# Attention and gated MLP in fp32 halves: weight words in PSUM, weight fetches among the first pairs' loads, value pooling on GpSimd

## The chip, the cores and the metric

The kernel runs on one core of a Trainium2 chip. A core has TensorE (PE, matrix products into PSUM), VectorE (DVE), ScalarE (ACT), GpSimd (POOL) and SyncE (SP), whose queue issues all transfers here; they work side by side and wait for each other by semaphores. The metric is the device time of one execution in microseconds (us), the median of the runs.

## The reference

Two stages. The attention, for 8 batches of 8 heads, 576 tokens, 64 wide:

```python
q_d = q.reshape(B, H, Sd, 4, D).mean(axis=3)        # k_d, v_d alike, Sd = 144
out_up = np.repeat(sm_attn(q_d, k_d, v_d), 4, axis=2)
mask = np.abs(pos[:, None] - pos[None, :]) < 4
scores = np.where(mask, scale * q @ k.T, -1e9)      # softmax over these, times v
out = out_up + out_local
```

The heads side by side are the rows x (8 x 576 tokens, 512 wide) of a gated MLP:

```python
xk = mu_k * x + (1 - mu_k) * x_prev                 # xr alike with mu_r; x_prev: the token before
k = np.maximum(xk @ w_k, 0.0)                       # 512 x 1024
v = (k * k) @ w_v                                   # 1024 x 512
out = v / (1 + np.exp(-(xr @ w_r)))                 # 512 x 512
```

The weights arrive as 64-bit floats and all else is fp32.

## The kernel before

*Attention* goes by pairs of heads, 32 of them, four to a batch (n = 0 to 31). SyncE loads q and k of a pair in four pieces each (`load_raw`, tag `raw`, four buffers), four-token groups of v (`load_v4`, two buffers) and windows of v (`load_windows`, three). VectorE transposes q and k (`turn_q`, `turn_k`), GpSimd pools them over four tokens (`pool_q`, `pool_k`, tiles `qd`, `kd`), and `pool_v` adds v over four tokens into `vd`: on VectorE for pairs below `VDVE`, else on GpSimd. PE writes local and pooled scores into one PSUM tile `ps_a`, VectorE takes maxima (`score_top`, `down_top`), ACT the exponentials, GpSimd the normalizations. PE then transposes the pooled weights (`down_turn`, "transpose group") and ACT spreads the local ones into `bd` (`spread`). `av_pe` multiplies with v, into the banks `acc0`, `acc1` for pairs 0 to 3 and into `c0`, `c1` after that, and VectorE adds both parts into `xt`, the rows x of a batch. From pair 5 on one block of PE work, `run_pe` ("run n"), holds the values of pair n-1 and the scores of pair n.

*The MLP* goes by chunks of 256 tokens, 18 of them (c = 0 to 17). Chunks 0 and 1 lie in batch 0, chunk 2 needs batch 1 too. `diff` forms x minus the token before (`dx`), ACT multiplies it with `mu_k` and `mu_r` (`mix_part`, tiles `muk`, `mur`, loaded by `load_mus`), VectorE adds x (`mix_add`) and splits each into a high and a low half (`xkh`, `xkl`, `xrh`, `xrl`). PE makes `k_pe` (8 k products per chunk), `r_pe` (2) and `v_pe` (8), each as three products of halves.

*The weights* come as 20 blocks of 128 x 512 64-bit floats (`WORDER`: k0 to k7, v0 to v7, r0 to r3). Each becomes an fp32 word and then two halves: ACT scales the upper 32 bits (`weight_scale`), VectorE shifts left by 3 (`weight_shift`), puts in the upper bits of the lower word (`weight_tail`) and the sign (`weight_sign`), ACT copies the high half (`weight_high`). The low half is made by PE and ACT for the first eight (`weight_diff` in a bank `c0` or `c1`, `weight_left`), by GpSimd for the others (`weight_low`). The word lies in the SBUF tile `w32`, tag `sig`, three buffers.

*The order* of the instructions on each engine is written out beforehand: `Plan` takes tasks with a duration, a rank and dependencies, and places them one by one, the task that can start first, among equals the lower rank. Buffers are handed out in the order in which the tasks were added. Each engine works through its list in that order, so a waiting instruction holds all behind it; SyncE's list is the order of the transfers. A weight's fetch has the rank

```python
add("SP", 0.5, FETCH + i, fetch_weight, i, w=[base], dma=1.75)      # FETCH = -95.0
```

and q and k of pair n the rank `at_run[n] - 18`, which is -94, -90, -86 and -82 for pairs 0 to 3.

Of the kernel before, what the change touches and what calls it, by code (L numbers as in the profile page):

```python
# [159 lines left out]
def attention_moe(ctx: ExitStack, tc, q, k, v, mu_k, mu_r, w_k, w_v, w_r, band, ident, out):  # L162
    nc = tc.nc
    cp = ctx.enter_context(tc.tile_pool(name="const", bufs=1))
    wp = ctx.enter_context(tc.tile_pool(name="work", bufs=2))
# [57 lines left out]


    def weight_scale(i):
        w = wp.tile([P, 512], F32, tag="sig", name="w32", bufs=3)
        nc.scalar.activation(w, raws[i][:, :, 1].bitcast(F32), AF.Copy, scale=2.0 ** -112)
        part32[i] = w

    def weight_shift(i):  # L230
        wi = part32[i].bitcast(I32)
        nc.vector.tensor_scalar(out=wi, in0=wi, scalar1=3, scalar2=None, op0=ALU.logical_shift_left)  # L232

    def weight_tail(i):
        wi = part32[i].bitcast(I32)
        nc.vector.scalar_tensor_tensor(out=wi, in0=raws[i][:, :, 0], scalar=29, in1=wi,  # L236
                                       op0=ALU.logical_shift_right, op1=ALU.bitwise_or)

    def weight_sign(i):
        wi = part32[i].bitcast(I32)  # L240
        nc.vector.scalar_tensor_tensor(out=wi, in0=raws[i][:, :, 1], scalar=-2147483648, in1=wi,  # L241
                                       op0=ALU.bitwise_and, op1=ALU.bitwise_or)
# [112 lines left out]
    def pool_v(n):  # L355
        d = st[n]
        v4 = d["v4"]
        vd = wp.tile([72, 4, D], F32, tag="vd", name="vd")
# [1 line left out]
        eng.tensor_tensor(out=v4[:, :, 0:128], in0=v4[:, :, 0:128], in1=v4[:, :, 128:256], op=ALU.add)  # L360
# [566 lines left out]
```

## Time and profile before

| | |
|---|---|
| Median of three runs | 721.09 us (720.60 to 721.62) |
| The profiled execution | 722.12 us, its span 720.3 us |
| Busy in the span | PE 657.7 us (91%), VectorE 489.1 (68%), ACT 439.4 (61%), GpSimd 299.7 (42%) |
| Moved | 62.2 MB, 85 GB/s over the span |
| A weight block, `v4` of a pair | 512 KB, 288 KB |
| Mean granted clock of PE | 0.955 |

The span runs from the first to the last instruction. "Busy" is the time in which an engine executed; idle time of an engine that nothing waits for costs nothing. A row of the timeline gives start, length, engine, line, operation, result and inputs, and in brackets the idle time before it and what ended it. Lines numbered L are those of the kernel before; after the change L222 is L223, L227 is L228, the three lines of shift, tail and sign keep their numbers (L232, L236, L241), and all behind them are three higher.

### The profile page before, as it was taken

Reading aid. Unit: us, or ns where it says so; the run is one execution under the profiler, and the core shown is the slowest. Engines: PE = TensorE matmul, PEld = TensorE weight load, DVE = VectorE, ACT = ScalarE, POOL = GpSimd, SP = SyncE. Lnnn points to the kernel's source line nnn. Section 1 sums busy time; section 2 is a strip of 40 time slices with the busy share of each in tenths; the row PEclk is TensorE's granted clock in tenths of the full one; section 3 lists DMA queues with packets and bytes.
Section 4 is the critical chain, followed back from the end, with each engine's and each line's share of the span. In section 5 each row is a group of like instructions: output and inputs, shape, how many; then the busy total and the mean of one; then the engine's idle time right before and its main releaser. Section 6 shows DMA issues by size and latency. Waiting matters only on the chain.

```text
span 720.3 us, 18419 instructions
## 1 busy us (share of the span) xinstructions
PE 657.7 (91%) x7352; PEld 567.0 (79%) x7352; DVE 489.1 (68%) x863; ACT 439.4 (61%) x1095; POOL 299.7 (42%) x366
## 2 busy tenths in 40 slices
PE   3557388699999999999999999999999999999997
PEld 2334276588888888888888888888888888988986
DVE  3676799987985887588764587667866774464111
ACT  3454457577675867596665667666766675644442
POOL 4233488866435455443343274434554431000000
PEclk9786589799999999999999999999999999999999
DMA  8999883456427343433243164432451100000000
GB/s 226 203 193 221 139 131 57 85 115 126 95 57 137 64 104 76 105 65 83 59 96 69 40 102 106 101 73 78 80 119 40 52 2 31 1 30 30 0 30 30
DMA packets 221848, 62.19 MB, mean 86 GB/s; under 512 B 205122, under 2 KB 214594, under 8 KB 221762
## 3 DMA queue, kind: packets, MB, share of 16 engines
q1 hardware_dynamic: 221762, 61.01, 40.5%
q8 instruction: 58, 0.95, 0.6%
q14 instruction: 28, 0.23, 0.1%
HBM read 51.55 MB, written 9.44 MB: 85 GB/s over the span
## 4 chain that ended last, share of the span: by engine, by line
PE 77%; DVE 9%; SPq 7%; DMA 4%; POOL 2%; issue 1%; ACT 1%; DVEq 0%; POOLq 0%; ACTq 0%
PE ps_g L615 26%; PE acc L664 26%; PE ps_r L646 14%; SPq L273 6%; DMA vw<-in_v_dram 3%; PE ps_v L519 3%; PE ps_a L387 3%; PE ps_v L513 2%; DVE w L241 1%; DVE w L236 1%; DVE w L232 1%; PE ps_a L454 1%; PE ps_a L447 1%; PE ps_t L494 1%; PE ps_t L495 1%
## 5 line engine op out<-in xcount | busy, mean ns | idle before, releaser
L615 PE MATMUL ps_g<-xkh,wk 128*128 128x256 f32 x1152 | 228.8, 285 | 2.2 <-ACT xkh L602 1.5
L615 PEld LDWEIGHTS ps_g<-xkh,wk 128*128 128x128 f32 x1152 | 186.9, 191 | 8.4 <-ACT xkh L602 2.0
L664 PE MATMUL acc<-wv,kh 128*128 128x512 f32 x576 | 182.2, 398 | 0.0
L615 PE MATMUL ps_g<-xkl,wk 128*128 128x256 f32 x576 | 163.1, 283 | 2.3 <-DVE xkl L607 2.3
L634 DVE TENSOR_TENSOR kl<-kk,kh 128x256 fp32r<-128x256 f32 x119 | 65.6, 552 | 104.2 <-ACT kh L627 96.4
L620 ACT ACTIVATE kk<-ps_g 128x256 f32<-128x256 f32 x144 | 54.8, 381 | 105.1 <-PE ps_g L615 102.4
L664 PEld LDWEIGHTS acc<-wv,kh 128*128 128x128 f32 x576 | 102.5, 190 | 17.1
L615 PEld LDWEIGHTS ps_g<-xkl,wk 128*128 128x128 f32 x576 | 109.5, 190 | 6.3 <-DVE xkl L607 2.6
L664 PE MATMUL acc<-wv,kl 128*128 128x512 f32 x288 | 113.7, 395 | 0.3 <-POOL kl L634 0.3
L646 PE MATMUL ps_r<-wr,xrh 128*128 128x512 f32 x288 | 90.0, 394 | 0.3 <-DVE sig L668 0.2
L664 PEld LDWEIGHTS acc<-wv,kl 128*128 128x128 f32 x288 | 54.5, 189 | 13.2 <-POOL kl L634 0.8
L627 ACT ACTIVATE kh<-kk 128x256 fp32r<-128x256 f32 x144 | 60.2, 418 | 4.6
L626 ACT ACTIVATE kk<-kk 128x256 f32<-128x256 f32 x144 | 60.1, 418 | 4.4
L634 POOL TENSOR_TENSOR kl<-kk,kh 128x256 fp32r<-128x256 f32 x25 | 22.1, 887 | 96.3 <-PE acc L664 81.5
L461 DVE TENSOR_REDUCE mxd<-ps_a 128x3 f32<-128x432 f32 x32 | 19.4, 606 | 62.7 <-PE ps_a L387 55.4
L646 PEld LDWEIGHTS ps_r<-wr,xrh 128*128 128x128 f32 x288 | 52.5, 188 | 10.5 <-DVE sig L668 0.6
L415 POOL TENSOR_TENSOR sm<-sm,mx 128x384 f32<-128x384 f32 x28 | 26.9, 959 | 79.5 <-DVE mx L410 68.1
L646 PE MATMUL ps_r<-wr,xrl 128*128 128x512 f32 x144 | 56.2, 390 | 0.0
L471 ACT ACTIVATE ad<-ps_a,mxd 128x144 f32<-128x144 f32 x96 | 35.3, 377 | 24.0 <-DVE mxd L462 12.1
L361 POOL TENSOR_TENSOR vd<-v 72x256 f32<-72x256 f32 x28 | 23.1, 824 | 62.6 <-PE ps_v L513 61.6
L351 POOL TENSOR_TENSOR tk<-kz 64x288 f32<-64x288 f32 (+1 forms) x56 | 44.4, 792 | 9.7 <-DVE kz L324 5.7
L482 POOL TENSOR_TENSOR ad<-ad,sd 128x432 f32<-128x432 f32 x32 | 29.8, 932 | 42.5 <-DVE sd L478 32.7
(105 smaller groups left out, 1212.1 us busy)
## 6 DMA issues: line engine op xcount, KB each, us to landing
vw<-in_v_dram SPq DMA_DIRECT2D x126, 96.0 KB
qraw<-in_q_dram SPq DMA_DIRECT2D x128, 72.0 KB
kraw<-in_k_dram SPq DMA_DIRECT2D x128, 72.0 KB
v<-in_v_dram SPq DMA_DIRECT2D x32, 288.0 KB
out_dram<-sig SPq DMA_DIRECT2D x36, 256.0 KB
wk<-in_moe_w_k_dram SPq DMA_DIRECT2D x8, 512.0 KB
wv<-in_moe_w_v_dram SPq DMA_DIRECT2D x8, 512.0 KB
wr<-in_moe_w_r_dram SPq DMA_DIRECT2D x4, 512.0 KB
```

Source lines behind the costliest of these rows:

```text
L273: nc.sync.dma_start(raw[o:o + 32], src[b, 2 * p + e].rearrange("(c t) (g d) -> t c g d", t=32, g=2)[:, :, dh, :])
L351: nc.gpsimd.tensor_tensor(out=tk[h], in0=k4[:, :, 0:2], in1=k4[:, :, 2:4], op=ALU.add)
L415: nc.gpsimd.tensor_tensor(out=s3, in0=s3, in1=mx[:, :, None].broadcast_to([P, 12, 32]), op=ALU.subtract)
L471: nc.scalar.activation(ad[:, t, :], ps[:, t, :], AF.Exp, scale=1.0 / 128, bias=mx[:, t:t + 1], accum_out=sd[:, t:t + 1])
L482: nc.gpsimd.tensor_tensor(out=ad, in0=ad, in1=sd[:, :, None].broadcast_to([P, 3, 144]), op=ALU.mult)
L615: nc.tensor.matmul(ps, w_k_part(p, f, w), y[:, p, :], start=(m == 0), stop=(m == len(mm) - 1))
L620: nc.scalar.activation(kk, kq[c, f], AF.Relu)
L626: nc.scalar.activation(kk, kk, AF.Square)
L627: nc.scalar.activation(kh, kk, AF.Copy)
L634: eng.tensor_tensor(out=kl, in0=kk, in1=kh.bitcast(F32), op=ALU.subtract)
L646: nc.tensor.matmul(ps, y[:, p, P * t:P * t + P], ws[f"r{p}"][:, w, :], start=(m == 0), stop=(m == len(mm) - 1))
L664: nc.tensor.matmul(accs[c][t], x[:, P * t:P * t + P], ws[f"v{f}"][:, w, :], start=(f == 0 and m == 0), stop=(f == NF - 1 and m == 2))
```

## The change

Three things. The word is built in PSUM: `weight_scale` writes to a PSUM tile in the bank `c0` or `c1` (by the weight's number), shift and tail work there, and `weight_sign` reads it and writes the finished word to `w32` in SBUF; `weight_diff` uses the same PSUM tile again. `Plan` lets the tiles of `c0`, `c1` and `sig` be handed out in the order in which it places the tasks (`ANY`), and takes the tail and the sign out of the list of work that slows beside GpSimd's. The ranks of the fetches are a list. And `VDVE = 0` puts all of `pool_v` on GpSimd.

```diff
-VDVE = 4
+VDVE = 0
-FETCH = -95.0
+FETCH = [-93.5, -93.0, -88.6, -88.5, -81.0, -80.9, -80.8, -80.7, -60, -59, -58, -57, -36, -35, -34, -33, -12, -11, -10, -9]
-    SHARED = "weight_tail weight_sign weight_low k_low mix_add mix_low mix_part diff pool_v".split()
+    SHARED = "weight_low k_low mix_add mix_low mix_part diff pool_v".split()
+    ANY = ("c0", "c1", "sig")
-                if tile not in self.queue[tag][turn[tag]:turn[tag] + same]:
+                if tag not in self.ANY and tile not in self.queue[tag][turn[tag]:turn[tag] + same]:
     def weight_scale(i):
-        w = wp.tile([P, 512], F32, tag="sig", name="w32", bufs=3)
-        nc.scalar.activation(w, raws[i][:, :, 1].bitcast(F32), AF.Copy, scale=2.0 ** -112)
-        part32[i] = w
+        shaped[i] = pp.tile([P, 512], F32, tag=w_bank(i), name="ps_w", bufs=1)
+        nc.scalar.activation(shaped[i], raws[i][:, :, 1].bitcast(F32), AF.Copy, scale=2.0 ** -112)
...
     def weight_sign(i):
-        wi = part32[i].bitcast(I32)
-        nc.vector.scalar_tensor_tensor(out=wi, in0=raws[i][:, :, 1], scalar=-2147483648, in1=wi,
-                                       op0=ALU.bitwise_and, op1=ALU.bitwise_or)
+        part32[i] = wp.tile([P, 512], F32, tag="sig", name="w32", bufs=3)
+        nc.vector.scalar_tensor_tensor(out=part32[i].bitcast(I32), in0=raws[i][:, :, 1], scalar=-2147483648,
+                                       in1=shaped[i].bitcast(I32), op0=ALU.bitwise_and, op1=ALU.bitwise_or)
+    def w_bank(i):
+        return f"c{i % 2}"
...
-        add("SP", 0.5, FETCH + i, fetch_weight, i, w=[base], dma=1.75)
-        add("ACT", 0.67, R, weight_scale, i, r=[base], new=[(f"w{i}", "sig")])
+        add("SP", 0.5, FETCH[i], fetch_weight, i, w=[base], dma=1.75)
+        add("ACT", 0.67, R, weight_scale, i, r=[base], new=[(f"ws{i}", w_bank(i))])
```

SyncE's queue behind the constants, before (`wk0` to `wr3` are weight blocks, `qraw`, `kraw`, `v4`, `vw` loads of the pairs in turn):

```order
L222 DMA wk0_91<-in_moe_w_k_dram 128x1024
L222 DMA wk1_94<-in_moe_w_k_dram 128x1024
L273 DMA qraw_96<-in_q_dram 32x18x32 x4
L273 DMA kraw_107<-in_k_dram 32x18x32 x4
L222 DMA wk2_114<-in_moe_w_k_dram 128x1024
L222 DMA wk3_117<-in_moe_w_k_dram 128x1024
L222 DMA wv0_122<-in_moe_w_v_dram 128x1024
L222 DMA wv1_124<-in_moe_w_v_dram 128x1024
L282 DMA v4_127<-in_v_dram 72x4x256
L273 DMA qraw_130<-in_q_dram 32x18x32 x4
```

and now:

```order
L276 DMA qraw_91<-in_q_dram 32x18x32 x4
L276 DMA kraw_101<-in_k_dram 32x18x32 x4
L223 DMA wk0_108<-in_moe_w_k_dram 128x1024
L223 DMA wk1_111<-in_moe_w_k_dram 128x1024
L285 DMA v4_113<-in_v_dram 72x4x256
L276 DMA qraw_118<-in_q_dram 32x18x32 x4
L276 DMA kraw_130<-in_k_dram 32x18x32 x4
L299 DMA vw_194<-in_v_dram 32x11x64
L303 DMA vw_194<-in_v_dram 29x64
L299 DMA vw_194<-in_v_dram 32x12x64 x3
L223 DMA wk2_212<-in_moe_w_k_dram 128x1024
L223 DMA wk3_217<-in_moe_w_k_dram 128x1024
```

Two weights stood ahead of pair 0's q and six ahead of pair 1's; now none and two.

SyncE's queue around `muk` and `mur`, before:

```order
L222 DMA wr2_488<-in_moe_w_r_dram 128x1024
L296 DMA vw_495<-in_v_dram 32x12x64 x4
L222 DMA wr3_515<-in_moe_w_r_dram 128x1024
L187 DMA muk_67<-in_moe_mu_k_dram 128x4x1
L188 DMA mur_68<-in_moe_mu_r_dram 128x4x1
L273 DMA qraw_537<-in_q_dram 32x18x32 x4
L273 DMA kraw_606<-in_k_dram 32x18x32 x4
L296 DMA vw_660<-in_v_dram 32x12x64 x4
```

and now:

```order
L223 DMA wv4_577<-in_moe_w_v_dram 128x1024
L223 DMA wv5_582<-in_moe_w_v_dram 128x1024
L223 DMA wv6_590<-in_moe_w_v_dram 128x1024
L223 DMA wv7_603<-in_moe_w_v_dram 128x1024
L188 DMA muk_67<-in_moe_mu_k_dram 128x4x1
L189 DMA mur_68<-in_moe_mu_r_dram 128x4x1
L276 DMA qraw_609<-in_q_dram 32x18x32 x4
L276 DMA kraw_685<-in_k_dram 32x18x32 x4
L223 DMA wr0_713<-in_moe_w_r_dram 128x1024
L223 DMA wr1_720<-in_moe_w_r_dram 128x1024
L223 DMA wr2_724<-in_moe_w_r_dram 128x1024
L223 DMA wr3_727<-in_moe_w_r_dram 128x1024
```

The r weights stand behind q and k of pair 4 and behind `muk` and `mur`, which stand behind the sixteen k and v weights still.

VectorE at the last weight word and chunk 1's `xk` (`at`: transposed local weights; `xt` rows: the values of pair 4), before:

```order
L232 TENSOR_SCALAR w32_1456<-w32_1456 128x512
L236 SCALAR_TENSOR_TENSOR w32_1456<-wr3_515,w32_1456 128x512
L241 SCALAR_TENSOR_TENSOR w32_1456<-wr3_515,w32_1456 128x512
L552 TENSOR_TENSOR xt_105<-ps_v_1308,up_1466 128x6x48
L552 TENSOR_TENSOR xt_105<-ps_v_1309,up_1466 128x6x48
L435 STREAM_TRANSPOSE at_1523<-sm_1427 128x384
L598 TENSOR_TENSOR xk32_1167<-xk32_1167,xt_101 128x1024
L310 STREAM_TRANSPOSE qT1_77<-qraw_1201 128x576
L319 STREAM_TRANSPOSE kz1_74<-kraw_1239 128x576
L607 TENSOR_TENSOR xkl_1626<-xk32_1167,xkh_1614 128x1024
```

and now (`ps_w` are the PSUM tiles):

```order
L232 TENSOR_SCALAR ps_w_1318<-ps_w_1318 128x512
L236 SCALAR_TENSOR_TENSOR ps_w_1318<-wr2_724,ps_w_1318 128x512
L241 SCALAR_TENSOR_TENSOR w32_1346<-wr2_724,ps_w_1318 128x512
L601 TENSOR_TENSOR xk32_1089<-xk32_1089,xt_97 128x1024
L232 TENSOR_SCALAR ps_w_1344<-ps_w_1344 128x512
L236 SCALAR_TENSOR_TENSOR ps_w_1344<-wr3_727,ps_w_1344 128x512
L241 SCALAR_TENSOR_TENSOR w32_1382<-wr3_727,ps_w_1344 128x512
L610 TENSOR_TENSOR xkl_1387<-xk32_1089,xkh_1372 128x1024
L601 TENSOR_TENSOR dx_997<-dx_997,xt_97 128x1024
L464 TENSOR_REDUCE mxd_1490<-ps_a_1390 128x3
```

The values of pair 4 and pair 5's `at` came before chunk 1's `xkl`; they come later now.

PE in front of chunk 1's first k product, before (`L513`, `L519`: values of pair 5; the rows of `ps_a`: scores of pair 6; its values' banks are `c0`, `c1`):

```order
L496 MATMUL ps_t<-idn,ad 72x2x16
L447 MATMUL ps_a<-kd,qd_69 128x144
L513 MATMUL ps_v<-adT,vd 64x144 x4
L519 MATMUL ps_v<-bd,vw 64x48 x24
L454 MATMUL ps_a<-kd,qd_69 64x144 x4
L392 MATMUL ps_a<-kz_73,qT_76 32x32 x48
L615 MATMUL ps_g<-xkh,wk_135 128x256
```

and now (values of pair 4, scores of pair 5, and the last v product of chunk 0):

```order
L667 MATMUL acc_1025<-wv_1245,kl 128x512
L450 MATMUL ps_a<-kd,qd_70 128x144
L516 MATMUL ps_v<-adT,vd 64x144 x4
L522 MATMUL ps_v<-bd,vw 64x48 x24
L457 MATMUL ps_a<-kd,qd_70 64x144 x4
L395 MATMUL ps_a<-kz_74,qT_77 32x32 x48
L667 MATMUL acc_1024<-wv_1278,kh 128x512 x2
L667 MATMUL acc_1024<-wv_1278,kl 128x512
L667 MATMUL acc_1025<-wv_1278,kh 128x512 x2
L667 MATMUL acc_1025<-wv_1278,kl 128x512
L618 MATMUL ps_g<-xkh,wk_210 128x256
```

One run fewer stands in front of that product, and the last v product stands behind the run; pair 6's run and its transpose group come after it.

More of the change, by code (lines that the diff above doesn't have):

```diff
@@ L203, in attention_moe @@
     wr, wk, wv = (x.bitcast(I32) for x in (w_r, w_k, w_v))
-    raws, ws, part32, left = {}, {}, {}, {}
+    raws, ws, shaped, part32 = {}, {}, {}, {}
     def weight_source(key):
@@ L225, in weight_scale @@
     def weight_scale(i):
-        w = wp.tile([P, 512], F32, tag="sig", name="w32", bufs=3)
-        nc.scalar.activation(w, raws[i][:, :, 1].bitcast(F32), AF.Copy, scale=2.0 ** -112)
-        part32[i] = w
+        shaped[i] = pp.tile([P, 512], F32, tag=w_bank(i), name="ps_w", bufs=1)
+        nc.scalar.activation(shaped[i], raws[i][:, :, 1].bitcast(F32), AF.Copy, scale=2.0 ** -112)
     def weight_shift(i):
-        wi = part32[i].bitcast(I32)
+        wi = shaped[i].bitcast(I32)
         nc.vector.tensor_scalar(out=wi, in0=wi, scalar1=3, scalar2=None, op0=ALU.logical_shift_left)
     def weight_tail(i):
-        wi = part32[i].bitcast(I32)
+        wi = shaped[i].bitcast(I32)
         nc.vector.scalar_tensor_tensor(out=wi, in0=raws[i][:, :, 0], scalar=29, in1=wi,
@@ L239, in weight_sign @@
     def weight_sign(i):
-        wi = part32[i].bitcast(I32)
-        nc.vector.scalar_tensor_tensor(out=wi, in0=raws[i][:, :, 1], scalar=-2147483648, in1=wi,
-                                       op0=ALU.bitwise_and, op1=ALU.bitwise_or)
+        part32[i] = wp.tile([P, 512], F32, tag="sig", name="w32", bufs=3)
[3 more added lines that the diff above has]
+        return f"c{i % 2}"
     def weight_high(i):
@@ L250, in weight_diff @@
         hi = ws[WORDER[i]][:, 0, :]
-        left[i] = ps = pp.tile([P, 512], F32, tag=f"c{i % 2}", name="ps_w", bufs=1)
+        ps = shaped[i]
         nc.tensor.matmul(ps, idn, part32[i], start=True, stop=False)
@@ L255, in weight_left @@
     def weight_left(i):
-        nc.scalar.activation(ws[WORDER[i]][:, 1, :], left[i], AF.Copy)
+        nc.scalar.activation(ws[WORDER[i]][:, 1, :], shaped[i], AF.Copy)
     def weight_low(i):
@@ L750, in weight @@
         base = "raw" + key
-        add("SP", 0.5, FETCH + i, fetch_weight, i, w=[base], dma=1.75)
-        add("ACT", 0.67, R, weight_scale, i, r=[base], new=[(f"w{i}", "sig")])
-        add("DVE", 0.66, R + 0.5, weight_shift, i, w=[f"w{i}"])
-        add("DVE", 0.95, R + 0.5, weight_tail, i, r=[base], w=[f"w{i}"])
-        add("DVE", 0.8, R + 0.5, weight_sign, i, r=[base], w=[f"w{i}"])
+        add("SP", 0.5, FETCH[i], fetch_weight, i, w=[base], dma=1.75)
+        add("ACT", 0.67, R, weight_scale, i, r=[base], new=[(f"ws{i}", w_bank(i))])
+        add("DVE", 0.6, R + 0.5, weight_shift, i, w=[f"ws{i}"])
+        add("DVE", 0.7, R + 0.5, weight_tail, i, r=[base], w=[f"ws{i}"])
+        add("DVE", 0.7, R + 0.5, weight_sign, i, r=[base, f"ws{i}"], new=[(f"w{i}", "sig")])
         add("ACT", 0.63, R + 2, weight_high, i, r=[f"w{i}"], w=["h" + key])
         if i in LOWPE:
-            add("PE", 1.5, R + 3, weight_diff, i, r=[f"w{i}", "h" + key, "nidn"], new=[(f"wd{i}", f"c{i % 2}")])
-            add("ACT", 0.64, R + 4, weight_left, i, r=[f"wd{i}"], w=["l" + key])
+            add("PE", 1.5, R + 3, weight_diff, i, r=[f"w{i}", "h" + key, "nidn"], w=[f"ws{i}"])
+            add("ACT", 0.64, R + 4, weight_left, i, r=[f"ws{i}"], w=["l" + key])
             return
```

## The prediction

> **What bounds the kernel now.** I read the page first: its busy tenths (40 slices of 18 us each).
>
> ```profile
> PE   3557388699999999999999999999999999999997
> DVE  3676799987985887588764587667866774464111
> DMA  8999883456427343433243164432451100000000
> ```
>
> PE is full from the ninth slice on and holes lie only in the first eight. So the kernel has a start-up of some 140 us and then runs as fast as TensorE does. Next I asked for busy times by stage.
>
> ```profile
> core 0: us, PE busy (x) PEld busy (x) DVE busy (x) ACT busy (x) POOL busy (x), PEclk, DMA share, GB/s
> 0.00:100.00 100.00, 51.89 (x872) 37.27 (x873) 69.25 (x117) 47.71 (x119) 41.13 (x59) 0.74 0.97 192
> 82.90:139.30 56.40, 39.47 (x585) 32.73 (x588) 55.54 (x59) 33.95 (x84) 47.02 (x43) 0.77 0.56 95
> 139.50:720.00 580.50, 576.29 (x6053) 505.75 (x6042) 381.18 (x702) 368.02 (x917) 224.08 (x276) 1.00 0.32 69
> ```
>
> After 139.5 us PE idles 4.2 us of 580.5. Before it two things end last: up to 80 us the transfers (DMA share 0.97 over the first 100 us, PE busy 52), then VectorE, busy 55.5 of the 56.4 us from 82.9 to 139.3. Half of that is weight words, as the same window for the tiles `w` on VectorE alone shows (24 instructions, 8 weights):
>
> ```profile
> 82.90:139.30 56.40, 28.13 (x24) 0.77 0.56 95
> ```
>
> That is 3.52 us a weight and leaves 27.4 us of other work. The answers by source line give VectorE's durations as min/median/max in ns:
>
> ```profile
> L232 DVE TENSOR_SCALAR w<-w x20: 384/423/1576, 7.0 to 130.3; 128x512 int32<-128x512 int32 x20
> L236 DVE SCALAR_TENSOR_TENSOR w<-wv,w x8: 680/798/3233, 27.2 to 111.3; 128x512 int32<-128x512 int32 x8
> L241 DVE SCALAR_TENSOR_TENSOR w<-wr,w x4: 798/1379/1676, 115.5 to 132.6; 128x512 int32<-128x512 int32 x4
> L409 DVE TENSOR_TENSOR sm<-ps_a,mask x28: 541/550/558, 89.6 to 599.1; 128x384 f32<-128x384 f32 x28
> L668 DVE TENSOR_TENSOR sig<-acc,sig x36: 627/679/693, 158.3 to 716.6; 128x512 f32<-128x512 f32 x36
> L461 DVE TENSOR_REDUCE mxd<-ps_a x32: 589/607/608, 18.2 to 596.9; 128x3 f32<-128x432 f32 x32
> ```
>
> The weight instructions, all from and to SBUF, stretch up to four times; the three lines that read PSUM (`ps_a`, `acc`) never vary by more than 0.07 us, though GpSimd was busy 47 of those 56 us.
>
> **The change, part by part.** *Words in PSUM.* The three VectorE instructions now read PSUM, the last two with one SBUF operand as in L668; its 0.68 us is the price of each (the shift has no second operand; L461's 0.607 at 432 elements, carried to 512, gives 0.69). A weight costs 2.04 us whatever GpSimd does. The bounds: 1.8 (the uncontended SBUF sum, 0.42+0.69+0.69), and 3.52+0.26=3.78 if contention stays and the shift grows from 0.42 to 0.68. I take 2.04, the nearest rows. ACT's scale to PSUM is bounded by its 0.66 now and 0.60 from PSUM; ACT is not full.
>
> [...]
>
> *Fetches by need.* Before, 19 weights go ahead of the last windows of batch 0 (pair 3's `vw`) and 20 ahead of `mur`; now 8 and 16. A weight takes 1.92 us, from the first two landings, which ACT waited for:
>
> ```profile
> 6.29 0.66 ACT L227 ACTIVATE w<-wk 128x512 f32<-128x512 f32 x1 [2.87 <-DMA wk<-in_moe_w_k_dram]
> 8.21 0.68 ACT L227 ACTIVATE w<-wk 128x512 f32<-128x512 f32 x1 [1.27 <-DMA wk<-in_moe_w_k_dram]
> 62.70 11.11 DMA vw<-in_v_dram
> 81.24 0.81 DVE L552 TENSOR_TENSOR xt<-ps_v,up 128x288 f32<-128x288 f32 x2
> 71.39 1.46 SPq L188 DMA_DIRECT2D mur<-in_moe_mu_r_dram  x1
> 79.97 0.78 DVE L310 STREAM_TRANSPOSE qT<-qraw 128x576 f32<-128x576 f32 x1 [4.07 <-DMA qraw<-in_q_dram]
> 84.24 1.71 ACT L584 ACTIVATE xk<-dx,muk 128x256 f32<-128x256 f32 x4 [1.41 <-POOL dx L573]
> 93.00 0.58 PE L615 MATMUL ps_g<-xkl,wk 128*128 128x256 f32 x1 [2.34 <-DVE xkl L607]
> ```
>
> The windows, issued last at 62.7, landed at 73.8 and batch 0's `xt` was complete at 82.0, 8.2 later. Now: 73.8 - 11x1.92 - 1.1 (one `v4` fewer ahead: 288 KB at a weight's 512 KB in 1.92 us) = 51.6, so `xt` at about 60, and `dx` about 2.5 us later. But `muk` and `mur` are still queued behind 16 weights. Their issue ended at 72.9; minus four weights and one `v4` (8.8) that is 64, and they land within the 7 us that pair 4's q took behind them: at 67. Pair 4's q lands at 79.97-8.8=71.2. So ACT's mixing starts at 67 (before: 84.2), VectorE adds `xk` at 68.8, then (at 70.0) waits 1.2 for q, which stands ahead of `xkl` in its order. Chunk 0's first k product comes near 74 instead of 93. Between 62 and 67 the wait for `mur` holds ACT's queue, with the scale of wk4 behind it, and VectorE behind that.
>
> *Value pooling on GpSimd.*
>
> ```profile
> L360 POOL TENSOR_TENSOR v<-v x28: 1263/1335/2267, 90.6 to 577.1; 72x512 f32<-72x512 f32 x28
> L360 DVE TENSOR_TENSOR v<-v x4: 648/684/689, 20.9 to 71.4; 72x512 f32<-72x512 f32 x4
> L361 POOL TENSOR_TENSOR vd<-v x28: 733/740/1595, 91.9 to 578.8; 72x256 f32<-72x256 f32 x28
> L361 DVE TENSOR_TENSOR vd<-v x4: 421/597/936, 21.7 to 72.1; 72x256 f32<-72x256 f32 x4
> ```
>
> It takes 4x1.3 us from VectorE and puts 4x2.1=8.4 us on GpSimd's queue, in front of the first pairs' normalizations, so `xt` can come that much later at most. Both lie before 67, under the wait for `mur`, which covers 4.5 of the 8.4; the price is 0 to 3.9, and I take 0, since `v4` lands before its pair needs it. Without that cover it would be paid in full.
>
> **The sum.** VectorE's work from the `xk` add to chunk 1's `xkl` is what 82.9 to 139.3 holds now, less what now comes later (pair 5's maxima, its sums, pair 4's `xt` and pair 5's `at`, pair 7's transposes), which one answer adds up over its four stretches:
>
> ```profile
> sum 7.76, DVE 7.59; mean DVE 1.90
> ```
>
> 27.4 - 7.6 + 1.5 (pair 4's transposes) = 21.3; twelve weights at 2.04 are 24.5; together 45.8. From 68.8+1.2 that ends at 115.8, and wr3's last word 1.2 (`xkl`) sooner, 114.6. That word matters: wr2 and wr3 hold the banks `c0` and `c1`, which pair 5's run needs for pair 4's values. So the run starts then. (A row with two times is a stretch with its length and PE's busy time: pair 8's run, and a group of transposes. The row behind them, of the chain of waits, is three v products.)
>
> ```profile
> 134.48 0.85 PE L447 MATMUL ps_a<-kd,qd 128*128 128x144 f32 x2 [4.91 <-POOL kd L352]
> 139.53 0.58 PE L615 MATMUL ps_g<-xkh,wk 128*128 128x256 f32 x1
> 154.74 1.02 PE L392 MATMUL ps_a<-kz,qT 64*32 64x32 f32 x96
> 164.60 0.96 ACT L441 ACTIVATE bd<-at,side 128x288 f32<-128x288 f32 x2 [1.23 <-DVE at L435]
> 165.32:168.21 2.89, 2.89 (x115) 1.00 0.63 105
> 175.26:175.89 0.63, 0.63 (x9) 1.00 0.00 0
> 171.29 4.13 PE acc L664 x18
> 184.51 0.28 PE L615 MATMUL ps_g<-xkh,wk 128*128 128x256 f32 x1
> ```
>
> Pair 6's run took 5.05 us (134.48 to 139.53), pair 8's 2.9 with PE full; I take 4 for this one and 1.4 (4.13/3) for a v product behind it, and chunk 1's first k product stands at 120.0 (before: 139.53). Chunk 2's first stands at 184.51, 45.0 later, on a full PE. In the new order pair 6's run, a transpose group and a v product (2.9+0.6+1.4) fall into that stretch: 49.9, to 169.9. And runs 8 and 9 now stand only two v products and a transpose group (3.4) apart. From the end of run 7 (155.8) to the tile `bd` that run 8 needs 1 us after its start (165.6) it took 9.8 us; so PE waits 9.8-1-3.4=5.4, and chunk 2 starts at 175.3. With the same work done the kernel now is at 184.5+1.4=185.9. The gain is 10.6 us; from there on both run full.
>
> The profiled program took 722.12 us for a span of 720.3, 1.0 over the median, 721.09; a gain of 10.6 gives a span of 709.7, 711.5 for its program, and 710.5 against the median, which I predict.
>
> **The rivals.** *Contention stays* (the other side). If a weight in PSUM costs 3.78, twelve cost 45.4, 20.9 more: 731.4. It decides at 10.6/12 more, 2.92 us a weight. For it: three SBUF-PSUM accesses a weight while GpSimd is as busy as now; against it L409 and L668. Chance 0.06; other ways to be slower (ACT or GpSimd's queue in the way of the words) 0.04.
>
> *The loads come later.* If `mur` and q lag by 8 us more, all behind them does: 718.5. For it: the DMA engines are full, nothing is moved fewer times, and the first pairs' small rows now come in one stretch with fewer weights between them. Against it: 8.8 us is what leaves the queue ahead of them. 0.13; and 0.05 that this and the waits eat the whole gain.
>
> *More is won.* These stretched too, behind GpSimd:
>
> ```profile
> 92.87 3.78 DVE L598 TENSOR_TENSOR dx<-dx,xt 128x1024 f32<-128x1024 f32 x1
> 141.42 1.21 DVE L598 TENSOR_TENSOR dx<-dx,xt 128x1024 f32<-128x1024 f32 x1
> L477 DVE TENSOR_SCALAR sd<-sd x32: 124/170/2559, 22.0 to 600.2; 128x3 f32<-128x3 f32 x32
> ```
>
> Chunk 0's `dx` took 3.78 where chunk 1's took 1.21, pair 4's `sd` 2.56 where 0.17 is usual: 5.0 us. If they go, 705.5, and without the wait before run 9, 700.1. Against it: GpSimd's work is not less. 0.14 for less than 704.
>
> **How the numbers follow.** The likeliest case, 0.58, lies between 704 and 716 (price per weight 1.8 to 2.5, `mur` 3 us either way). The range takes in the most of more won and the late loads, 699 to 719, and leaves out the slower cases and the tip of the gain. What this kernel can tell from no change is 0.2%, 1.4 us. Faster 0.85, same 0.05, slower 0.10.
>
> **What would show it.** The weight lines within 0.1 us of 0.68, none over 0.8; ACT's first mixing at 64 to 71, waiting for `mur`; chunk 0's k at 71 to 78; chunk 1's at 115 to 125 with pair 5's run just behind wr3's last word; a PE hole of some 5 us before run 9. I am wrong if a weight takes 3 us, if `mur` lands after 75, or if the first pairs' `xt` come later than 67.

## The result, and the profile after

The changed kernel takes 714.92 us (median of four runs, 713.55 to 716.55), the kernel before 721.02 beside it: a ratio of 0.9922, 95% interval 0.9897 to 0.9947. Measured again later, with more runs, it took 714.19 against 720.34 (0.9904, 0.9881 to 0.9927). The forecast was 710.5 with 699 to 719 about it. So the sign and the range held, and 6 of the 10.6 us came.

The profiled execution after took 714.58 us for a span of 712.8. Its busy tenths, of the page (slices of 17.8 us), and its stages around the first products of chunks 0, 1 and 2, by windows (column names in the first line; the first window runs from chunk 0's `xk` add to the end of chunk 1's `xkl`, both on VectorE):

```profile
PE   3576768997999999999999999999999999999997
DVE  3764999749766887588852797577867874464111
DMA  7899886554435343424142173434351100000000
```

```profile
core 0: us, PE busy (x) PEld busy (x) DVE busy (x) ACT busy (x) POOL busy (x), PEclk, DMA share, GB/s
71.30:114.20 42.90, 32.67 (x415) 26.80 (x415) 41.52 (x59) 35.74 (x82) 33.05 (x34) 0.87 0.80 159
115.78:176.18 60.40, 53.06 (x778) 44.22 (x776) 43.92 (x79) 37.02 (x100) 37.65 (x49) 0.93 0.56 108
176.18:712.80 536.62, 531.39 (x5440) 467.66 (x5436) 343.20 (x638) 335.25 (x830) 197.66 (x240) 1.00 0.29 65
```

TensorE's row now reaches its nines in the eighth slice, not the ninth, and dips once more in the tenth. VectorE is still the busy one from the xk add (71.3) to chunk 1's xkl (114.2): 41.5 of 42.9 us. The weight words in it, by source line (min/median/max in ns) and as the sum over the same window for VectorE's instructions on the tiles `ps_w`:

```profile
L232 DVE TENSOR_SCALAR ps_w<-ps_w x20: 662/689/700, 11.8 to 110.0; 128x512 int32<-128x512 int32 x20
L236 DVE SCALAR_TENSOR_TENSOR ps_w<-wr,ps_w x4: 696/697/697, 101.1 to 110.7; 128x512 int32<-128x512 int32 x4
L241 DVE SCALAR_TENSOR_TENSOR w<-wr,ps_w x4: 648/687/689, 102.2 to 111.5; 128x512 int32<-128x512 int32 x4
71.30:114.20 42.90, 24.22 (x36) 0.87 0.80 159
```

Twelve weights (36 instructions) cost 24.22 us, 2.02 each, where eight cost 28.13 before. None of these instructions stretches any more. The start of the chain, rows of the timeline (start, length, idle time before and its cause in brackets):

```profile
65.18 0.81 DVE L555 TENSOR_TENSOR xt<-ps_v,up 128x288 f32<-128x288 f32 x2
69.56 1.70 ACT L587 ACTIVATE xk<-dx,muk 128x256 f32<-128x256 f32 x4 [2.31 <-DMA muk<-in_moe_mu_k_dram]
75.71 0.58 PE L618 MATMUL ps_g<-xkl,wk 128*128 128x256 f32 x1 [1.32 <-DVE xkl L610]
112.22 0.84 PE L522 MATMUL ps_v<-bd,vw 64*64 64x48 f32 x42 [0.30 <-DVE w L241]
115.78 0.28 PE L618 MATMUL ps_g<-xkh,wk 128*128 128x256 f32 x1
```

Batch 0's `xt` is complete at 66.0 (before 82.0), the mixing waits for `muk` until 69.6, chunk 0 multiplies at 75.7 (before 93.0), and chunk 1 at 115.8 (before 139.5). That is 23.8 us sooner; at chunk 2 it is 8.3 (176.18 against 184.51), and at the end 7.5. Between chunk 1 and run 8 TensorE is busy 40.2 of 42.3 us, and no wait stands in front of runs 6, 7 and 8 (the first three rows). Behind run 8 comes this hole:

```profile
130.09 0.41 PE L450 MATMUL ps_a<-kd,qd 128*128 128x144 f32 x2
143.10 0.41 PE L450 MATMUL ps_a<-kd,qd 128*128 128x144 f32 x2
158.12 0.41 PE L450 MATMUL ps_a<-kd,qd 128*128 128x144 f32 x2
167.69 0.43 PE L497 MATMUL ps_t<-idn,ad 128*72 128x128 f32 x1 [3.66 <-POOL ad L485]
169.90 0.85 PE L450 MATMUL ps_a<-kd,qd 128*128 128x144 f32 x2 [0.79 <-ACT adT L506]
172.67 1.59 PE L522 MATMUL ps_v<-bd,vw 64*64 64x48 f32 x47 [0.77 <-ACT bd L444]
173.12 1.23 DVE L610 TENSOR_TENSOR xkl<-xk,xkh 128x1024 fp32r<-128x1024 f32 x1
176.18 0.58 PE L618 MATMUL ps_g<-xkh,wk 128*128 128x256 f32 x1
```

Run 8 (158.12) is followed by two v products; then TensorE waits for pair 8's normalized weights, for their copy and for `bd`, 5.2 us in all. It has nothing else to do: chunk 2's `xkl`, which needs pair 7's values of run 8, is ready at 174.4.

One comparison runs through all that follows. Chunk 2's first k product and the time of the same execution, of every trace of this study (us; "from chunk 2 on" is the execution less chunk 2's start):

| kernel | mixing starts | chunk 0, first with xkl | chunk 1, first k | run 8 | chunk 2, first k | execution | from chunk 2 on |
|---|---|---|---|---|---|---|---|
| before | 84.24 | 93.00 | 139.53 | 165.32 | 184.51 | 722.12 | 537.6 |
| changed | 69.56 | 75.71 | 115.78 | 158.12 | 176.18 | 714.58 | 538.4 |
| words only | 88.06 | 99.19 | 127.12 | 164.87 | 182.98 | 725.84 | 542.9 |
| fetches only | 69.22 | 75.04 | 138.51 | 164.34 | 183.62 | 721.81 | 538.2 |
| pooling only | 90.88 | 100.74 | 135.59 | 162.01 | 181.21 | 719.33 | 538.1 |
| words and fetches | 69.16 | 76.91 | 126.07 | 153.44 | 172.77 | 710.94 | 538.2 |
| same order, pooling on VectorE | 67.64 | 73.80 | 113.85 | 155.96 | 174.00 | 712.12 | 538.1 |
| other order, pooling on GpSimd | 70.95 | 78.71 | 128.38 | 155.75 | 175.08 | 713.26 | 538.2 |
| muk, mur sooner | 66.12 | 73.30 | 113.27 | 156.97 | 175.01 | 713.66 | 538.7 |
| 32 dummies | 68.52 | 74.67 | 114.72 | 156.83 | 176.14 | 714.72 | 538.6 |
| changed, again | 70.03 | 76.19 | 116.67 | 158.67 | 176.61 | 714.81 | 538.2 |
| 16 dummies | 69.88 | 76.03 | 116.50 | 158.42 | 176.42 | 714.58 | 538.2 |
| run 8 sooner | 69.14 | 75.29 | 115.33 | 154.92 | 173.27 | 711.52 | 538.3 |
| combined | 67.45 | 74.69 | 114.68 | 154.19 | 172.70 | 710.95 | 538.3 |

Behind chunk 2's first k product a kernel takes 537.6 to 538.7 us, whatever came before (the one exception, words only, is an execution 5 us above the median of its kernel). So the question for every edit is when chunk 2 starts. Run 8 says most of that: chunk 2 follows it by 17.9 to 19.3 us in all fourteen. The columns further left say little. Each row is one execution, and executions of one kernel differ: pooling only and before, equal by their medians below, lie 3.3 us apart at chunk 2 here.

### The profile page after: what moved, and what is told of

Same layout as the page of the kernel before. It is cut to its first block, busy times and chain, and to the rows that moved or that the text cites. A ratio compares the mean times of both kernels' runs of the same rounds, so it can differ in the third digit from the quotient of the medians.

```text
span 712.8 us, 18403 instructions
## 1 busy us (share of the span) xinstructions
PE 658.3 (92%) x7352; PEld 565.4 (79%) x7352; DVE 470.3 (66%) x855; ACT 438.7 (62%) x1095; POOL 300.2 (42%) x374
## 4 chain that ended last, share of the span: by engine, by line
PE 76%; DVE 9%; SPq 6%; DMA 5%; ACT 1%; issue 1%; POOL 0%; DVEq 0%; ACTq 0%; POOLq 0%
PE ps_g L618 26%; PE acc L667 25%; PE ps_r L649 14%; SPq L276 4%; PE ps_v L522 3%; PE ps_a L390 3%; PE ps_v L516 2%; DMA muk<-in_moe_mu_k_dram 1%; DMA wk<-in_moe_w_k_dram 1%; DMA vw<-in_v_dram 1%; SPq L299 1%; DVE ps_w L236 1%; PE ps_a L457 1%; DMA qraw<-in_q_dram 1%; DVE ps_w L232 1%
## 5 line engine op out<-in xcount | busy, mean ns | idle before, releaser
L418 POOL TENSOR_TENSOR sm<-sm,mx 128x384 f32<-128x384 f32 x28 | 28.7, 1025 | 83.6 <-DVE mx L413 72.2
L637 POOL TENSOR_TENSOR kl<-kk,kh 128x256 fp32r<-128x256 f32 x25 | 20.5, 820 | 99.4 <-PE acc L667 81.4
L363 POOL TENSOR_TENSOR v<-v 72x512 f32<-72x512 f32 x32 | 45.5, 1421 | 20.7 <-DMA v<-in_v_dram 20.6
L354 POOL TENSOR_TENSOR tk<-kz 64x288 f32<-64x288 f32 (+1 forms) x56 | 43.1, 771 | 10.6 <-DVE kz L327 5.4
```

The costliest lines, as they stand in the source:

```text
L354: nc.gpsimd.tensor_tensor(out=tk[h], in0=k4[:, :, 0:2], in1=k4[:, :, 2:4], op=ALU.add)
L418: nc.gpsimd.tensor_tensor(out=s3, in0=s3, in1=mx[:, :, None].broadcast_to([P, 12, 32]), op=ALU.subtract)
L637: eng.tensor_tensor(out=kl, in0=kk, in1=kh.bitcast(F32), op=ALU.subtract)
```

## The experiments

**The three parts alone.** Each was made by itself in the kernel before, and words and fetches together.

*Words only*: the changed kernel with the fetches and the pooling of before.

```diff
-VDVE = 0
+VDVE = 4
-FETCH = [-93.5, -93.0, -88.6, -88.5, -81.0, ...
+FETCH = [-95.0 + i for i in range(20)]
```

> Theory (the words' contention was the price, the loads only set when the work can start): only the words move to PSUM; fetches and value pooling stay as before, so xk cannot start before about 84 us. The weight lines on VectorE fall to 0.68 us each with none over 0.8. Eight weights stood between 82.9 and 139.3, each 1.48 us cheaper, so chunk 1's first k product comes up to 11.8 us sooner (near 128), and 4 to 9 us of that arrive at the end: 712 to 717. Rival 1 (the order of the loads made the whole gain): 720 to 722. Rival 2 (the words made the whole gain): 714 to 716, the same as the changed kernel.

Measured: 720.65 against 720.94, ratio 1.0004 (0.9989 to 1.0020). No gain; my theory gave 712 to 717. The time is rival 1's, whose reason the next run refutes. The words did become as cheap as forecast (the three lines of the weights read 0.63 to 0.70), and chunk 1 came 12.4 us sooner, but from chunk 1 to chunk 2 it took 55.9 us and not 45.0. In part that is the order: run 6 stands behind chunk 1's first product here (132.1) and stood in front of it before (134.5). Run 8 starts at 164.87, before at 165.32, so the lead was gone by then. At the start VectorE, early with its words, stood at a load (the first row), and chunk 0 came 6.2 us later than before:

```profile
90.41 0.78 DVE L313 STREAM_TRANSPOSE qT<-qraw 128x576 f32<-128x576 f32 x1 [2.91 <-DMA qraw<-in_q_dram]
127.12 0.28 PE L618 MATMUL ps_g<-xkh,wk 128*128 128x256 f32 x1
182.98 0.38 PE L618 MATMUL ps_g<-xkh,wk 128*128 128x256 f32 x1
```

*Fetches only*: the kernel before with the list of ranks.

```diff
-FETCH = -95.0
+FETCH = [-93.5, -93.0, -88.6, -88.5, -81.0, ...
-        add("SP", 0.5, FETCH + i, fetch_weight, ...
+        add("SP", 0.5, FETCH[i], fetch_weight, ...
```

> Theory: xk starts near 67 to 70 as in the changed kernel, but twelve weights still to be shaped in SBUF at 3.5 us each plus 21 us of other work keep VectorE until about 134, and chunk 1's first k product stands at 136 to 140: 717 to 721. The weight lines still stretch to 1.4 us and more. Rival 1 (the loads alone made the gain): 714 to 716 and chunk 1's k at 116. Rival 2 (the new order of fetches costs where the words are not faster): over 722.

Measured: 720.98 against 720.94, ratio 1.0003 (0.9991 to 1.0016). As the theory said. Mixing starts at 69.22 and chunk 0 multiplies at 75.0, 18 us sooner, and then VectorE needs 59.5 of 63.5 us, 39.7 of them for twelve words (the second line: the tiles `w` alone), until chunk 1 starts at 138.5:

```profile
69.22 1.69 ACT L584 ACTIVATE xk<-dx,muk 128x256 f32<-128x256 f32 x4
75.04:138.51 63.47, 43.95 (x592) 35.31 (x592) 59.45 (x69) 36.80 (x90) 51.16 (x47) 0.78 0.60 108
75.04:138.51 63.47, 39.70 (x35) 0.78 0.60 108
138.51 0.58 PE L615 MATMUL ps_g<-xkh,wk 128*128 128x256 f32 x1
```

That is 3.3 us a word in SBUF, beside 2.02 in PSUM.

*Pooling only*: one constant of the kernel before.

```diff
-VDVE = 4
+VDVE = 0
```

> Theory: value pooling of the first four pairs moves under the loads and changes nothing at the end: 720 to 722. Rival (GpSimd's queue, which then waits for each v4 load ahead of the normalizations, delays the first pairs): 723 to 725, with chunk 0's first k product 2 to 4 us later than 93.0.

Measured: 720.53 against 720.94, ratio 0.9999 (0.9985 to 1.0013). Nothing at the end, as the theory said; the rival was right that the start comes later (chunk 0 at 100.7, not 93.0, more than its 2 to 4 us), but that cost nothing.

*Words and fetches*: the same constant, set back in the changed kernel.

```diff
-VDVE = 0
+VDVE = 4
```

> The changed kernel with value pooling of pairs 0 to 3 back on VectorE. Theory: nothing at the end depends on it, 714 to 716; chunk 0's first k product within 1 us of 73.8, because muk and mur come last there. Rival (waits for v4 on GpSimd hold the normalizations of the first pairs, and that is part of what the gain lacks): 711 to 713, with the first mixing on ScalarE 2 to 4 us before 69.6.

Measured: 712.37 against 720.94, ratio 0.9886 (0.9869 to 0.9904), that is 8.6 us. Neither text held: the time is the rival's, its mechanism is not, since the mixing starts only 0.4 us sooner than in the changed kernel.

So two edits that gain nothing alone gain 8.6 us together. The loads decide when the work can begin (mixing at 69 us, before at 84) and VectorE's words how long it takes (2.02 us each, in SBUF 3.3); with one of them left, chunk 2 starts at 183 to 184. And the third edit seems to take some of it back.

**Does the pooling cost, or the order that the planner writes with it?** The planner writes another order for pooling on VectorE (run 6 at 120 and not 130). So order and engine were crossed: `pool_v` asks a second constant for its engine, and the planner keeps its own.

```diff
-VDVE = 0
+VDVE, ONDVE = 0, 4          # and 4, 0 in the crossed case
-        eng = nc.vector if n < VDVE else nc.gpsimd
+        eng = nc.vector if n < ONDVE else nc.gpsimd
```

> The changed kernel with its own order of instructions kept, but the value pooling of pairs 0 to 3 executed on VectorE. Words plus fetches with the planner's own order for pooling on VectorE took 712.4, 2.5 us less than the changed kernel. Theory A (the 2.5 us lie in the other order that the planner writes, runs 5 to 8 standing 4 to 10 us earlier): this kernel takes 714 to 716, and run 8 starts within 1.5 us of 158.1. Theory B (GpSimd's queue, which waits for v4, costs them): 711.5 to 713.5, run 8 at 154 to 156.

Measured: 712.32 against 720.5, ratio 0.9889 (0.9874 to 0.9903). Theory B. Four runs gave 712.1 to 713.3, ten of the changed kernel 712.8 to 716.6 (median 714.7); the intervals of the ratios overlap, so the 2.4 us between these medians are likely, not certain. The traces show one place. With pooling on GpSimd pair 3's normalization, whose sums VectorE has ready at 52.9, stands in GpSimd's queue behind the wait for that pair's `v4` and its pooling, until 57.62:

```profile
52.70 0.18 DVE L481 RECIPROCAL sd<-sd 128x3 f32<-128x3 f32 x1
55.60 1.26 POOL L363 TENSOR_TENSOR v<-v 72x512 f32<-72x512 f32 x1 [6.58 <-DMA v<-in_v_dram]
57.62 0.91 POOL L485 TENSOR_TENSOR ad<-ad,sd 128x432 f32<-128x432 f32 x1
```

With pooling on VectorE it starts at 54.93, 0.2 us behind its sums, and batch 0's `xt` is complete at 63.5 and not 66.0. But in both kernels the mixing waits for `muk` (issue on SyncE's queue and start of the mixing, the changed kernel first):

```profile
59.42 0.85 SPq L188 DMA_DIRECT2D muk<-in_moe_mu_k_dram  x1
69.56 1.70 ACT L587 ACTIVATE xk<-dx,muk 128x256 f32<-128x256 f32 x4 [2.31 <-DMA muk<-in_moe_mu_k_dram]
```

```profile
56.81 0.39 SPq L188 DMA_DIRECT2D muk<-in_moe_mu_k_dram  x1
67.64 1.71 ACT L587 ACTIVATE xk<-dx,muk 128x256 f32<-128x256 f32 x4 [1.14 <-DMA muk<-in_moe_mu_k_dram]
```

Why `muk` is issued 2.6 us sooner with pooling on VectorE is not shown. A buffer of `v4` does not explain it: there are two, so pair 3's load waits for pair 1's pooling, and GpSimd had done that by 30.7, while the load was issued at 45.26 (42.62 with pooling on VectorE). The difference grows from 0.4 us at pair 1's k to 2.4 at pair 2's windows, ahead of that load. In the five traces of kernels that share the changed kernel's start the mixing begins between 68.5 and 70.0; 67.64 lies outside of that.

> The crossed case: the order that the planner writes for pooling on VectorE, with the pooling executed on GpSimd all the same. Theory A (the order matters): 711.5 to 713.5, with run 6 near 120 and chunk 2's first k product near 171 to 173. Theory B (the engine matters): 714 to 716, chunk 2 near 175 to 177.

Measured: 713.03, ratio 0.9894 (0.9881 to 0.9907), 0.7 us above the same order with the pooling on VectorE, less than the runs can tell apart. The time is theory A's, chunk 2 (175.08 in an execution of 713.26) theory B's. So the price of the pooling is up to 2.4 us in the one order and not shown in the other: the two theories are not exclusive, and how they share the difference stays open.

**muk and mur sooner**: the order kept, the one task moved.

```diff
     emitted = plan.order()
+    mus = next(t for t in emitted if t["name"] == "load_mus")
+    emitted.remove(mus)
+    emitted.insert(1 + next(i for i, t in enumerate(emitted) if t["name"] == "load_windows" and t["args"] == (3,)), mus)
```

> The changed kernel with muk and mur issued right behind pair 3's windows, ahead of the last eight weight blocks, all else in its order. The wait of ScalarE for muk (2.31 us before the mixing at 69.56) goes: mixing starts when dx ends, near 68. Theory A (VectorE is full from there to chunk 1, so an earlier start is an earlier end): chunk 0's k near 72, chunk 1's near 114, 712.5 to 714. Theory B (the pairs' loads, later by the small rows' time, or the latency of pairs 5 to 8 end last whatever the start): 714.5 to 716.

Measured: 713.66, ratio 0.9905 (0.9891 to 0.9919), about 1 us below the changed kernel and not told apart from it, though inside theory A's range. Mixing starts at 66.12 and waits for `dx` alone; chunk 1 comes 2.5 us sooner (113.27), chunk 2 only 1.2 (175.01). Half of what is won at the start is lost by run 8 (156.97, 1.2 us sooner).

**The half clock.** Around run 9 the granted clock is 0.50 (windows from 168 to 177), and run 9 takes 6.3 us, 0.8 of them a wait for `bd`, where run 8 takes 2.9 at a clock of 1.00. Dummy products of the identity were put into the hole ahead of pair 8's transposes.

```diff
             d["ps_t"] = [ps[0:72, 512 * kt:512 * kt + 288] for kt in range(2)]
+            for _ in range(WARM.get(n, 0)):          # WARM = {8: 32}, then {8: 16}
+                nc.tensor.matmul(ps[:, 512:640], idn, idn, start=True, stop=True)
```

> The changed kernel with 32 dummy products of the identity in the hole of 3.66 us ahead of pair 8's transposes, into a part of PSUM that the transposes use afterwards; the output is unchanged. Theory (the hole costs twice, once as idle time and once as the clock of 0.50 that TensorE has from 167.7 to 177.9): the granted clock stays at 1.00, run 9 takes 4 to 5 us instead of 6.3 (it still waits for bd), chunk 2's first k product comes near 174.8 and 2 to 3 us are won: 711.5 to 713. Rival 1 (chunk 2's xkl at 174.35 and the work behind it set the time, the cold clock cost nothing): 714 to 716. Rival 2 (the dummies delay the transposes): over 716.

Measured: 716.0, ratio 0.9935 (0.9921 to 0.9949): no gain, on the edge of the second rival. A dummy is two records of 0.115 us, so that the 32 filled 7.4 us and not the hole, and the transposes came 2.3 us later. ScalarE's copy of them stands ahead of `bd` in its order, so run 9 got `bd` 17.3 us behind the start of run 8, and 14.55 in the changed kernel. But TensorE did not fall to half clock there: 46 of its products with `bd` took 0.95 us (first row), where 47 take 1.59 in the changed kernel at a clock of 0.50. What is left of run 9 behind `bd` took 2.0 us, where the changed kernel takes 3.5 (172.67 to 176.18):

```profile
174.13 0.95 PE L525 MATMUL ps_v<-bd,vw 64*64 64x48 f32 x46 [1.44 <-ACT bd L445]
176.14 0.38 PE L621 MATMUL ps_g<-xkh,wk 128*128 128x256 f32 x1
```

Together chunk 2 came 19.3 us behind run 8 and not 18.1, and the median is as much, 1.3 us, above the changed kernel's (714.7). The profiled execution, with run 8 at 156.83, is the fastest of the six.

> The dummy products again, 16 in place of 32. In the longer version a dummy took 0.20 us and not 0.11, the 32 ran until 170.5 and pushed run 9 from 169.9 to 171.5, so the clock of 1.00 that they kept was paid for. 16 of them take 3.2 us and fit the hole of 3.66. Theory (the half clock from 167.7 to 177.9 costs 2 to 3 us at the end): 711.5 to 713. Rival (chunk 2's xkl, ready at 174.4, and bd, ready at 172.6, end last, so the clock costs less than 1.5): 713.5 to 715.5.

Measured: 714.0, beside 714.19 for the changed kernel in the same set (0.9903, 0.9881 to 0.9924, against 0.9904). The time is the rival's. The 16 took 3.8 us, 0.24 each and not 0.20, and filled the hole. The rows of TensorE, and two windows:

```profile
164.31 3.81 PE L497 MATMUL ps_t<-idn 128*128 128x128 f32 x32
172.97 1.59 PE L525 MATMUL ps_v<-bd,vw 64*64 64x48 f32 x47 [2.04 <-ACT bd L445]
168.00:172.00 4.00, 1.97 (x20) 1.44 (x18) 3.93 (x9) 3.62 (x9) 1.29 (x2) 1.00 0.35 131
172.00:176.00 4.00, 3.03 (x93) 2.65 (x97) 3.94 (x5) 1.93 (x6) 3.69 (x6) 0.61 0.59 96
```

The clock stayed at 1.00 up to 172, TensorE got sooner to the wait for `bd`, waited 2.04 us there instead of 0.77, and fell to half clock in that wait. `bd` came 14.55 us behind run 8, as without dummies: time moved from one wait into the next. And the rest of run 9 behind `bd` took 3.45 us, at a clock of 0.52. So this run took the half clock away only where a wait covers it, and does not say that it costs nothing. My estimate from the two lengths above is 1.5 us at chunk 2's start (3.5 less 2.0); no run with this order of run 8 and run 9 had both a `bd` in time and a clock of 1.00 behind it.

The changed kernel itself ran once more in that set.

> The changed kernel once more, beside the next three, since these lie within a few us of it: 713.5 to 716.5.

Measured: 714.19 (712.81 to 715.36), ratio 0.9904 (0.9881 to 0.9927).

**Run 8 sooner.** Only the order changes: chunk 1's last k product and one v product go behind run 8, and what follows from that k product behind pair 8's exponentials. TensorE's list around it, before and after the edit:

```diff
 L667 MATMUL acc_2028<-wv_1091,kl 128x512
+L450 MATMUL ps_a<-kd,qd_69 128x144
+L516 MATMUL ps_v<-adT,vd 64x144 x4
+L522 MATMUL ps_v<-bd,vw 64x48 x24
+L457 MATMUL ps_a<-kd,qd_69 64x144 x4
+L390 MATMUL ps_a<-kz_73,qT_76 32x64 x24
 L618 MATMUL ps_g<-xkh,wk_963 128x256
...
 L667 MATMUL acc_2028<-wv_1171,kl 128x512
-L450 MATMUL ps_a<-kd,qd_69 128x144
...
```

> The changed kernel, where run 8 stands ahead of chunk 1's last k product and one v product (2.84 us of TensorE work) and not behind them; what follows from that k product moves behind pair 8's exponentials. Nothing else moves. Theory (the gain was given back between run 8 and chunk 2, where TensorE has too little work for the latency of pair 7's xt and pair 8's weights): run 8 starts at 155.6 in place of 158.1, the hole of 3.66 us shrinks to about 1, the clock stays at 1.00, and chunk 2's first k product comes at 171.5 to 174 in place of 176.2: 710 to 712.5. Rival (the wait only moves to the next pairs, so that nothing arrives at the end): 714 to 716.

Measured: 711.87 against 720.34, ratio 0.9877 (0.9853 to 0.9902), 2.3 us below the changed kernel beside it. The intervals overlap; the four runs (711.3 to 713.2) lie below five of the six of the changed kernel. The time and chunk 2 (173.27) are the theory's, the clock is not, it fell all the same, to 0.50 from 166.7 on:

```profile
154.92 0.41 PE L450 MATMUL ps_a<-kd,qd 128*128 128x144 f32 x2
164.94 0.30 PE L497 MATMUL ps_t<-idn,ad 128*72 128x128 f32 x1 [1.34 <-POOL ad L485]
169.93 1.59 PE L522 MATMUL ps_v<-bd,vw 64*64 64x48 f32 x47 [1.18 <-ACT bd L444]
173.27 0.39 PE L618 MATMUL ps_g<-xkh,wk 128*128 128x256 f32 x1
```

Against the changed kernel run 8 starts 3.2 us sooner and chunk 2 2.9, though chunk 1 came only 0.5 sooner.

**Combined**: words and fetches, the changed kernel's order with the pooling of pairs 0 to 3 on VectorE, `muk` and `mur` behind pair 3's windows, run 8 sooner; the edits are those above.

```diff
-VDVE = 0
+VDVE, ONDVE = 0, 4
...
+    emitted.insert(1 + next(i for i, t in enumerate(emitted) if t["name"] == "load_windows" and t["args"] == (3,)), mus)
...
+    emitted[at["k_pe", (1, 7)]:last8 + 1] = out8      # run 8 ahead of k_pe(1, 7) and v_pe(1, 5)
```

> Words in PSUM and fetches by need, in the changed kernel's order, with value pooling of pairs 0 to 3 on VectorE (2.6 us less alone), muk and mur behind pair 3's windows (1.3 less alone) and run 8 sooner. Theory (the first two start the same chain sooner and overlap in part, the third closes a hole behind it): mixing at 65 to 66.5, chunk 2's first k product at 168 to 171, 707.5 to 710.5. Rival (they all relieve the same wait): 711 to 712.5.

Measured: 710.72 against 720.34, ratio 0.9861 (0.9836 to 0.9886). The fastest median of the study, 3.5 us below the changed kernel beside it, between the two ranges, and by its places nearer the rival (mixing 67.45, forecast 65 to 66.5): the mixing starts 1.7 us sooner than with run 8 alone, chunk 2 only 0.6 (172.70). The three gains, 5.7 us by their medians (2.4, 1.0, 2.3), do not add up.

## Why the prediction was right, and where it was not

*The price of a word* (2.04 a weight): right, 2.02 measured, no instruction over 0.70, with GpSimd busy 33 of 43 us. The counterpart is fetches alone: there the same three instructions, with the word in SBUF, took 3.3 a weight, with GpSimd busy 51 of 63 us. *Contention stays* is refuted.

*The loads* (`xt` at 60, mixing at 67, chunk 0 at 74): 66.0, 69.6, 75.7, 1.7 to 6 us late. `muk` ended the wait, the first of the two loads that I had put last. Of `xt`'s 6 us up to 4.7 are pair 3's normalization in GpSimd's queue (above), which the wait for `muk` covered. "The loads come later" was a small part of the truth, not the 8 us of the rival.

*The price of the pooling*, 0 to 3.9, taken as 0: likely too small. The argument, that `v4` lands before its pair needs it, was false, as the group of the page shows (busy, mean ns, and idle time before with its cause; all of it before the first four pairs):

```profile
L363 POOL TENSOR_TENSOR v<-v 72x512 f32<-72x512 f32 x32 | 45.5, 1421 | 20.7 <-DMA v<-in_v_dram 20.6
```

The cover that the sum counted on held all the same: `dx` was done at 68.0 and the mixing waited for `muk` until 69.6. The crossing gives up to 2.4 us in this order; with it came an earlier `muk`, for which the sum has no term and these traces no cause.

*Chunk 1 at 120.0*: 115.8. VectorE's other work took 17.3 us (41.5 less 24.2) and not 21.3. This is *more is won*, which came for the most part: the two instructions that it named, chunk 0's `dx` add and pair 4's `sd`, took 1.22 and 0.88 us and not 3.78 and 2.56, 4.2 of its 5.0.

```profile
75.58 1.22 DVE L601 TENSOR_TENSOR dx<-dx,xt 128x1024 f32<-128x1024 f32 x1
96.54 0.88 DVE L480 TENSOR_SCALAR sd<-sd 128x3 f32<-128x3 f32 x1
```

The stretching did not go away, it fell elsewhere: chunk 1's `dx` add, just behind this stretch, took 3.01 us where it took 1.21. Run 5 did not wait for the last word to start: it began at 110.6, 4.0 sooner than in the sum, behind other products, and only its values waited for the bank (0.30). From there to chunk 1 it was 5.2 us, forecast 5.4.

*Chunk 2 at 175.3*: 176.2, and here two errors nearly cancel, which was luck: chunk 1 came 4.2 us sooner than in the sum, and from there to chunk 2 it took 60.4 us and not 55.3. The terms of the sum put run 8 40.7 us behind chunk 1, and chunk 2 14.6 behind run 8 (2.9 + 2.8 + 0.6 + 5.4 + 2.9); measured were 42.3 and 18.1. The difference lies in three places:

- Up to run 8, 1.6 us: TensorE waited 2.1 us where the sum has it full, 1.66 of them for ScalarE's `kk` at 120.39.
- From run 8 to `bd`, 1.7 us: from the end of run 8 (161.1) it took 11.5 us to `bd`, where the sum took over 9.8 from run 7 of the kernel before. Pair 8's weights were normalized at 169.7, but VectorE transposed them only from 171.1, behind chunk 2's `xk` add and a transpose of q.
- Behind `bd`, 1.5 us: the rest of run 9 took 3.5 us at half clock, and 2.0 with the 32 dummies. The sum let TensorE come out of a wait of 5.4 us at full clock.

The three are 4.8 of the 5.1 us. The waiting before and in run 9 came out as forecast (5.2 against 5.4) because the longer way to `bd` and the half clock before it, which spreads TensorE's work over the wait (run 9's products ahead of `bd` took 2.0 us, run 8's 1.05 at a clock of 1.00), offset each other. I treated the stretch as TensorE's work plus one wait. Behind run 8 it was a latency with TensorE's work inside: an earlier end of that work is worth nothing before `bd` is there, while a run 8 that stood 3.2 us sooner gave 2.9.

*"From there on both run full"*: not quite. From chunk 2 on the sum had 537.6 less 1.4 us for work already done, 536.2; it took 538.4. So 2.2 us went there. 0.85 of them is half clock until 177.9 (531.4 us busy for what should be 530.5, the 531.9 of before less 1.4), the rest is this wait:

```profile
201.79 0.30 PE L497 MATMUL ps_t<-idn,ad 128*72 128x128 f32 x1 [1.38 <-POOL ad L485]
```

Against the forecast for the program, 711.5, the profiled 714.58 is 3.1 longer: 0.9 up to chunk 2 and 2.2 behind it. The other 1.3 between 710.5 and 714.92 come from the medians: I took 1.0 off for the profiled run of before, and the one after lay 0.3 below its median.

Two things stay open: why `muk` is issued sooner with the pooling on VectorE, and why words alone gain nothing though chunk 1 came 12 us sooner. In that trace run 8 came 0.5 us sooner, so it was lost before run 8; the execution was the longest of its twelve.

## What to carry to other kernels

Two limits that overlap in a start-up hide each other: here cheaper words and sooner loads each gave nothing and together 8.6 us, so test them together before dropping either. Find the point behind which all versions take the same time (here chunk 2's first product), and follow back the chain that ends there; an earlier start of something else is worth only what reaches it. Where an engine takes over a small step, ask what the step waits for and what stands behind it in that engine's queue: here a normalization stood 4.7 us behind a load that it did not need. And before products are added to keep the clock up, find the one that the chain waits for: here the clock counted only behind `bd`, by the estimate above.
